# Attention block with a query projection: the first eight heads' queries accumulated chunk by chunk, six heads at once

## The chip, the cores and the metric

The kernel runs on one core of a Trainium2 chip. The metric is the time of one execution in device microseconds; smaller is better. Besides timed executions there is, for each kernel, one profiled execution with its trace. The profile's span (first to last instruction) is about 1.8 us shorter than the time of the same execution. All times in the profile count from the start of the span.

## The reference, cut to what matters

Two independent problems, A and B, of the same shape, and their results side by side:

```python
# x: (16, 32, 1024)   wq: (1024, 32*128)   k_cache, v_cache: (16, 4, 512, 128)   wo: (32*128, 1024)
q = (x @ wq)                         # 32 query heads of 128
scores = q @ k.T * 128 ** -0.5       # 8 query heads share one of 4 key/value heads
o = softmax(scores) @ v
out = o @ wo
```

All is bfloat16. Only the very first step of problem A matters here: x transposed (512 tokens by 1024 model dimensions, in 8 chunks of 128 dimensions), and heads 0 to 7 of `x @ wq`. Each head takes 8 matmuls, one for each chunk, of 128 x 128 weights against 512 token columns.

## The kernel before: the parts that matter

TensorE works through one long stream. In a start phase it transposes x and projects heads 0 to 7. Then come 128 slots, each with one score group, one value group and about seven matmuls of a background stream (`units`): the other heads' projections, later the output projection. The background starts with four matmuls of head 8 before the first slot.

```python
load_x(0); load_x(1)                                   # 128 tokens each, 256 KB
load_first_wq(slice(0, 2 * DH), slice(0, HC))          # heads 0, 1: chunks 0-3, 256 KB
load_first_wq(slice(0, 2 * DH), slice(HC, DC))         # heads 0, 1: chunks 4-7
load_x(2); load_x(3)
load_first_wq(slice(2 * DH, 4 * DH), slice(0, DC))     # heads 2, 3
load_wq(0, 1)                                          # heads 4-7, 1 MB
load_k(0); load_v(0); load_wq(0, 2); load_k(1); load_v(1)
...
warm_up(5)                                             # dummy matmuls while x is on its way
transpose_x(0); transpose_x(1)
first_q = [psum.tile([P, NW], FP32, name="q_ps", tag="proj") for _ in range(2)]
warm_up(2)
for dcs in (lower, upper):                             # heads 0, 1 on the first 256 tokens
    for h in range(2):
        first_heads(h, 0, 2, dcs)
transpose_x(2); transpose_x(3)
for h in range(2):
    for tt in (2, 3):                                  # ... and on 128 tokens at a time
        first_heads(h, tt, tt + 1, range(DC))
...                                                    # two copies out of PSUM
units = stream()                                       # heads 2, 3, ... one after another
run(units, (REP - 2) * DC + 4)                         # heads 2-7 and four matmuls of head 8
...
for i in range(total_slots + 3):                       # slot i: loads of the plan, scores(i), ...
```

## Time and profile before

| | |
|---|---|
| time, median (lowest to highest of 3) | 350.49 us (349.77 to 350.71) |
| span of the profile | 348.6 us |
| TensorE (PE) busy | 98% of the span |
| first score group (first slot) starts | 22.56 us |
| last copy of the output starts (ScalarE) | 344.38 us |
| x, in four loads, has landed | 3.5, 4.2, 7.8, 8.8 us |

The page's chain of waits, followed back from the last instruction, has shares of the span by engine. It is nearly all TensorE:

```profile
PE 96%; DMA 2%; SPq 1%; DVE 1%; issue 0%; ACT 0%
```

Here is the start in the timeline: start us, duration us, engine, line, operation, what it writes and reads, and how many; in brackets the idle time before and what ended it. L491 are dummy matmuls, L506 transposes of x, L516 heads 0 and 1, L312 heads 2 and up, L371 scores, L341 the last copy.

```profile
1.29 2.32 PE L491 MATMUL warm_ps<-warm 128*128 128x512 bf16 x5 [1.29 <-DVE warm L230]
3.55 1.56 PE L506 MATMUL xT_ps<-ident,x_sb 128*128 128x128 bf16 x16
...
5.76 1.92 PE L516 MATMUL q_ps<-xT,wq_sb 128*128 128x256 bf16 x16 [0.21 <-DMA wq_sb<-in_A_wq_dram]
...
7.81 0.62 PE L506 MATMUL xT_ps<-ident,x_sb 128*128 128x128 bf16 x8
...
8.88 0.62 PE L506 MATMUL xT_ps<-ident,x_sb 128*128 128x128 bf16 x8 [0.45 <-DMA x_sb<-in_A_x_dram]
...
9.34 2.11 PE L516 MATMUL q_ps<-xT,wq_sb 128*128 128x128 bf16 x32
...
11.34 11.38 PE L312 MATMUL q_ps<-xT,wq_sb 128*128 128x512 bf16 x52
...
22.56 0.60 PE L371 MATMUL s_ps<-qT,kT 128*128 128x256 bf16 x4
...
344.38 0.37 ACT L341 CAST o_sb<-f_ps 128x256 bf16<-128x256 f32 x1 [22.13 <-PE f_ps L331]
```

From 11.34 us on TensorE has hardly a gap. What comes before holds waits for x and for weights, and 48 narrow matmuls for two heads. A matmul of 512 columns starts every 0.216 us at full speed (52 of them take 11.38 us, of which the last one's own latency is 0.38), and a dummy one at the start every 0.42 us: the array still runs at half its rate there.

### The profile page before, as it was taken

How to read it: one execution, taken by the hardware profiler on the slowest of the kernel's cores; microseconds unless marked ns; L12 is line 12 of the kernel's file. 1: busy time of each engine (PE TensorE's matmuls, PEld its weight loads, DVE VectorE, ACT ScalarE, POOL GpSimd, SP SyncE). 2: the span in 40 equal slices, each digit the busy share in tenths (PEclk: the TensorE clock that was granted, in tenths of full speed). 3: DMA queues.
4: the chain of work that ended last, by engine and by line, in shares of the span. 5: the costliest groups of instructions: out<-in, count | busy, mean ns of one | idle time of the engine just before them, and what ended most of it. 6: DMA issues, size and time to landing. Idle time of an engine off the chain costs nothing.

```text
span 348.6 us, 5527 instructions
## 1 busy us (share of the span) xinstructions
PE 342.2 (98%) x2217; PEld 221.2 (63%) x2217; DVE 282.6 (81%) x420; ACT 180.4 (52%) x197; POOL 8.9 (3%) x21
## 2 busy tenths in 40 slices
PE   7999999999999999999999999999999999999995
PEld 4556666666666666666666666666666666666554
DVE  2118988888988889898889989999999999899710
ACT  3347667666666766666654454454455445445000
POOL 0000000000000000000000000000000000000010
PEclk9999999999999999999999999999999999999999
DMA  7999999899997899999999459995589995400000
GB/s 224 240 302 333 168 253 270 241 276 256 270 253 197 172 249 222 311 267 268 279 316 222 115 124 270 349 212 121 137 259 263 252 227 102 120 18 0 15 32 20
DMA packets 125069, 71.70 MB, mean 206 GB/s; under 512 B 73616, under 2 KB 124048, under 8 KB 125040
## 3 DMA queue, kind: packets, MB, share of 16 engines
q1 hardware_dynamic: 124176, 69.29, 81.7%
q0 software_dynamic: 720, 1.97, 1.7%
q8 instruction: 18, 0.29, 0.3%
q14 instruction: 11, 0.09, 0.1%
q10 hardware_dynamic: 144, 0.07, 0.1%
HBM read 51.38 MB, written 2.10 MB: 153 GB/s over the span
## 4 chain that ended last, share of the span: by engine, by line
PE 96%; DMA 2%; SPq 1%; DVE 1%; issue 0%; ACT 0%
PE f_ps L331 32%; PE q_ps L312 31%; PE ob L431 16%; PE s_ps L371 16%; DMA x_sb<-in_A_x_dram 2%; PE q_ps L516 1%; SPq L468 0%; DVE parts L390 0%; PE sums L407 0%; SPq L471 0%; DVE o_sb L343 0%; PE xT_ps L506 0%; ACT o_sb L341 0%; DVE cs L399 0%; PE ok_ps L627 0%
## 5 line engine op out<-in xcount | busy, mean ns | idle before, releaser
L379 ACT ACTIVATE p_sb<-s_ps,shift 128x1024 bf16<-128x1024 f32 x128 | 142.5, 1113 | 113.1 <-PE s_ps L371 100.4
L390 DVE TRANSPOSE_TENSOR_REDUCE parts<-p_sb 128x32 f32<-128x1024 bf16 x128 | 158.2, 1236 | 22.1 <-ACT p_sb L379 21.6
L331 PE MATMUL f_ps<-wo_sb,oT 128*128 128x512 bf16 (+1 forms) x544 | 133.3, 367 | 0.0
L312 PE MATMUL q_ps<-xT,wq_sb 128*128 128x512 bf16 x496 | 129.6, 380 | 0.0
L371 PE MATMUL s_ps<-qT,kT 128*128 128x256 bf16 x512 | 76.8, 273 | 0.0
L431 PE MATMUL ob<-p_sb,v_sb 128*128 128x256 bf16 x512 | 76.8, 273 | 0.0
L331 PEld LDWEIGHTS <-oT 128*128 128x128 bf16 x544 | 53.0, 98 | 33.8
L312 PEld LDWEIGHTS <-wq_sb 128*128 128x128 bf16 x496 | 48.4, 98 | 34.7 <-DMA wq_sb<-in_A_wq_dram 0.3
L371 PEld LDWEIGHTS <-kT 128*128 128x128 bf16 x512 | 56.9, 113 | 20.9
L431 PEld LDWEIGHTS <-v_sb 128*128 128x128 bf16 x512 | 50.1, 98 | 19.8 <-DVE oT L453 0.2
L453 DVE TENSOR_TENSOR oT<-r,ob 128x512 bf16<-128x512 f32 x64 | 43.9, 685 | 12.8 <-PE ob L431 9.4
L418 DVE STREAM_TRANSPOSE r<-rall 128x512 f32<-128x512 f32 x64 | 45.5, 711 | 2.2
L320 ACT CAST qT<-q_ps 128x512 bf16<-128x512 f32 x62 | 36.1, 583 | 21.3 <-PE q_ps L312 19.2
L407 PE MATMUL sums<-cs,fold 128*128 128x16 f32 x64 | 22.9, 357 | 0.1
L343 DVE CAST o_sb<-f_ps 128x512 bf16<-128x512 f32 (+1 forms) x16 | 10.8, 673 | 10.8 <-PE f_ps L331 10.0
L399 DVE TENSOR_REDUCE cs<-parts 128x16 fp32r<-128x64 f32 x64 | 16.8, 262 | 2.2
L407 PEld LDWEIGHTS sums<-cs,fold 128*128 128x128 f32 x64 | 12.1, 190 | 8.3 <-DVE cs L399 0.9
L345 POOL DMA_DIRECT2D out_dram<-o_sb x15 | 8.2, 549 | 329.3 <-DVE o_sb L343 298.6
L416 DVE RECIPROCAL rall<-sums 128x16 f32<-128x16 f32 x64 | 14.1, 220 | 0.0
L341 ACT CAST o_sb<-f_ps 128x256 bf16<-128x256 f32 x1 | 0.4, 372 | 22.1 <-PE f_ps L331 22.1
L509 DVE COPY xT<-xT_ps 128x512 bf16<-128x512 bf16 x4 | 1.7, 424 | 5.6 <-PE xT_ps L506 5.6
L509 ACT COPY xT<-xT_ps 128x512 bf16<-128x512 bf16 x4 | 2.3, 585 | 5.7 <-PE xT_ps L506 5.7
(27 smaller groups left out, 24.1 us busy)
## 6 DMA issues: line engine op xcount, KB each, us to landing
v_sb<-in_A_v_cache_dram SPq DMA_DIRECT2D x16, 512.0 KB, 5.0
wq_sb<-in_B_wq_dram SPq DMA_DIRECT2D x8, 1024.0 KB, 6.5
wo_sb<-in_A_wo_dram SPq DMA_DIRECT2D x8, 1024.0 KB, 7.6
v_sb<-in_B_v_cache_dram SPq DMA_DIRECT2D x16, 512.0 KB, 4.5
wo_sb<-in_B_wo_dram SPq DMA_DIRECT2D x8, 1024.0 KB, 8.8
wq_sb<-in_A_wq_dram SPq DMA_DIRECT2D x7, 1024.0 KB, 7.4
out_dram<-o_sb POOLq DMA_DIRECT2D x15, 128.0 KB, 3.6
x_sb<-in_A_x_dram SPq DMA_DIRECT2D x4, 256.0 KB, 3.9
```

Of the source, the lines that this page charges most:

```text
L312: nc.tensor.matmul(ps[:], lhsT=w[:, dc, (h % 4) * DH:(h % 4 + 1) * DH], rhs=xT[pr][:, dc, :], start=(dc == 0), stop=(dc == DC - 1),)
L320: nc.scalar.copy(out=qT[pr, g][:, :, hl, :], in_=ps[:].rearrange("p (b s) -> p b s", s=SQ),)
L331: nc.tensor.matmul(ps[:, 0:width], lhsT=oT[pr, tt][:, h, :], rhs=wo_tiles[pr, nh, h // REP][:, h % REP, off:off + width], start=(h == 0), ...
L371: nc.tensor.matmul(s_ps[:, c, :], lhsT=kT[:, i % GRP, c, :], rhs=qT[pr, g][:, b, :, :].rearrange("p h s -> p (h s)"), start=True, stop=True,)
L379: nc.scalar.activation(out=p_sb[:], in_=s_ps[:], func=ACTF.Exp, bias=shift[:], scale=SCALE)
L390: nc.vector.tensor_reduce(out=parts[j][:, q, :, :].rearrange("p c h -> p (c h)"), in_=st[i]["p"][:].rearrange("p c (h s) -> p (c h) s", s=SQ),
L399: nc.vector.tensor_reduce(out=cs[:], in_=parts.pop(j)[:].rearrange("p q c h -> p q h c"), axis=AX.X, op=ALU.add,)
L407: nc.tensor.matmul(sums[:], lhsT=fold[:].rearrange("p r s -> p (r s)"), rhs=cs[:].rearrange("p q h -> p (q h)"), start=True, stop=True,)
L416: nc.vector.reciprocal(out=rall[:, j, :], in_=pair.pop(j)[:])
L418: nc.vector.transpose(out=r[:].rearrange("p n s -> p (n s)"), in_=rall[:, j, :].unsqueeze(2).to_broadcast([P, 2 * REP, SQ]),)
L431: nc.tensor.matmul(ob[j][:, q, :], lhsT=v_sb[:, i % GRP, c, :], rhs=st[i]["p"][:, c, :], start=(c == 0), stop=(c == KC - 1),)
L453: nc.vector.tensor_tensor(out=out, in0=rcp.pop(j)[:].rearrange("p (q h) s -> p q h s", h=REP), in1=ob.pop(j)[:].rearrange("p q (h s) -> p ...
```

## The change

The intent: no head should wait for all of x. The loads come in chunks of the model dimension, two chunks of x and then the weights of all eight heads for one chunk at a time, and six heads advance together in six PSUM banks, so that each 256 KB of weights feeds six full-width matmuls as soon as it lands. The other two banks serve the transposes. Heads 6 and 7 follow when the transposes are done. The diff, cut to its core, with comments added:

```diff
-            load_x(0)
-            load_x(1)
-            load_first_wq(slice(0, 2 * DH), slice(0, HC))
-            load_first_wq(slice(0, 2 * DH), slice(HC, DC))
-            load_x(2)
-            load_x(3)
-            load_first_wq(slice(2 * DH, 4 * DH), slice(0, DC))
-            load_wq(0, 1)
-            load_k(0)
-            load_v(0)
-            load_wq(0, 2)
+            load_x(0, slice(0, TT // 2))            # two chunks of x, half of the tokens: 128 KB
+            load_x(0, slice(TT // 2, TT))
+            load_w0(0, slice(0, HALF * DH))         # chunk 0 of the weights, heads 0-3: 128 KB
+            load_w0(0, slice(HALF * DH, REP * DH))
+            for k in range(1, DC // 2):
+                load_x(k)                           # 256 KB each from here
+                load_w0(2 * k - 1)
+                load_w0(2 * k)
+            load_w0(DC - 1)
+            load_k(0, slice(0, 1))
+            load_wq(0, 2)
+            load_k(0, slice(1, GRP))
+            load_v(0)
             load_k(1)
             load_v(1)
...
-            warm_up(5)
...
+            warm_up(4)
+            transpose_x(0)                          # now chunks 2k and 2k+1, all tokens
+            warm_up(1, QW)
...                                                  # first_q: six banks
+            for dc in range(DC - 2):
+                for h in range(NF):                 # NF = 6
+                    first_head(first_q[h], h, dc)
+                if dc % 2 == 0:
+                    transpose_x(dc // 2 + 1)
+            for h in (0, 2, 4, 1, 3, 5):
+                for dc in (DC - 2, DC - 1):
+                    first_head(first_q[h], h, dc)
+                evacuate(first_q[h], h)
...                                                  # heads 6 and 7, all chunks; VectorE copies head 7
-            run(units, (REP - 2) * DC + 4)
+            run(units, 4)
```

From the first slot on both kernels issue the same work in the same order.

More of the change, by code (lines that the diff above doesn't have):

```diff
@@ L279, in kv_part, with load_k @@
                 return t[jj]
-            def load_k(j):
+            def load_k(j, qs=slice(0, GRP)):
                 ks = kv_part(j, 1)
-                kT = k_tiles[j] = kv.tile([P, GRP, SK], BF16, name="kT")
+                if qs.start == 0:
+                    k_tiles[j] = kv.tile([P, GRP, SK], BF16, name="kT")
+                kT = k_tiles[j]
                 if j < NG // GRP:
-                    for q in range(GRP):
+                    for q in range(qs.start, qs.stop):
                         nc.sync.dma_start_transpose(out=kT[:, q, :], in_=ks[q])
@@ L463, in fast_path @@
             wq_v = A_wq.rearrange("(c p) n -> p c n", p=P)
-            wq_tiles[0, 0] = blk_tile([P, DC, 4 * DH], "wq_sb")
             HC = DC // 2
-            def load_x(tt):
-                nc.sync.dma_start(out=x_sb[:, tt, :], in_=x_v[:, tt, :])
-            def load_first_wq(ns, cs):
-                nc.sync.dma_start(out=wq_tiles[0, 0][:, cs, ns], in_=wq_v[:, cs, ns])
-            load_x(0)
-            load_x(1)
-            load_first_wq(slice(0, 2 * DH), slice(0, HC))
-            load_first_wq(slice(0, 2 * DH), slice(HC, DC))
@@ L477, in fast_path, with load_x, load_w0 @@
-            load_x(2)
-            load_x(3)
-            load_first_wq(slice(2 * DH, 4 * DH), slice(0, DC))
-            load_wq(0, 1)
-            load_k(0)
+            w0 = [blk_tile([P, HC, REP * DH], "w0_sb") for _ in range(2)]
+            def load_x(k, ts=slice(0, TT)):
+                cs = slice(2 * k * P, (2 * k + 2) * P)
+                nc.sync.dma_start(out=x_sb[:, ts, cs], in_=x_v[:, ts, cs])
+            def load_w0(dc, ns=slice(0, REP * DH)):
+                nc.sync.dma_start(out=w0[dc // HC][:, dc % HC, ns], in_=wq_v[:, dc, ns])
@@ L485, in fast_path, with warm_up @@
             load_v(1)
-            warm_ps = psum.tile([P, NW], FP32, name="warm_ps", tag="sums", bufs=1)
-            def warm_up(n):
+            warm_ps = psum.tile([P, NW], FP32, name="warm_ps", tag="proj")
+            def warm_up(n, width=NW):
                 for _ in range(n):
                     nc.tensor.matmul(
-                        warm_ps[:], lhsT=warm[:, 0:P], rhs=warm[:], start=True, stop=True
+                        warm_ps[:, 0:width], lhsT=warm[:, 0:P], rhs=warm[:, 0:width],
+                        start=True, stop=True,
@@ L493, in warm_up @@
                     )
             xT[0] = blk_tile([P, DC, NTOK], "xT")
-            def transpose_x(tt):
-                ts = slice(tt * P, (tt + 1) * P)
-                bank = ("ob", "proj", "sums", "ob")[tt]
-                for cs, where_, copy in (
-                    (slice(0, HC), dict(tag="s"), nc.vector.tensor_copy),
-                    (slice(HC, DC), dict(tag=bank, bufs=2 if bank == "proj" else 1), nc.scalar.copy),
-                ):
-                    xT_ps = psum.tile([P, HC, P], BF16, name="xT_ps", **where_)
-                    for k, dc in enumerate(range(cs.start, cs.stop)):
-                        nc.tensor.transpose(
-                            xT_ps[:, k, :], x_sb[:, tt, dc * P:(dc + 1) * P], ident[:]
-                        )
-                    copy(out=xT[0][:, cs, ts], in_=xT_ps[:])
@@ L511, in fast_path @@
-            qT[0, 0] = blk_tile([P, B, REP, SQ], "qT")
-            def first_heads(h, t0, t1, dcs):
-                ts = slice(t0 * P, t1 * P)
-                for dc in dcs:
-                    nc.tensor.matmul(
-                        first_q[h][:, ts],
-                        lhsT=wq_tiles[0, 0][:, dc, h * DH:(h + 1) * DH],
-                        rhs=xT[0][:, dc, ts],
-                        start=(dc == 0),
-                        stop=(dc == DC - 1),
-                    )
-            lower, upper = range(HC), range(HC, DC)
@@ L525, in fast_path @@
-            warm_up(5)
-            transpose_x(0)
-            transpose_x(1)
-            first_q = [psum.tile([P, NW], FP32, name="q_ps", tag="proj") for _ in range(2)]
-            warm_up(2)
-            for dcs in (lower, upper):
-                for h in range(2):
-                    first_heads(h, 0, 2, dcs)
-            transpose_x(2)
-            transpose_x(3)
-            for h in range(2):
-                for tt in (2, 3):
-                    first_heads(h, tt, tt + 1, range(DC))
@@ L538, in fast_path, with transpose_x @@
-            for h, copy in enumerate((nc.vector.tensor_copy, nc.scalar.copy)):
+            def transpose_x(k):
+                ps = [
+                    psum.tile([P, NTOK], BF16, name="xT_ps", tag=tag, bufs=1)
+                    for tag in ("ob", "sums")
+                ]
+                for ts in (range(0, TT // 2), range(TT // 2, TT)):
+                    for o in range(2):
+                        dc = 2 * k + o
+                        for tt in ts:
+                            nc.tensor.transpose(
+                                ps[o][:, tt * P:(tt + 1) * P],
+                                x_sb[:, tt, dc * P:(dc + 1) * P],
+                                ident[:],
+                            )
+                nc.vector.tensor_copy(out=xT[0][:, 2 * k, :], in_=ps[0][:])
+                nc.scalar.copy(out=xT[0][:, 2 * k + 1, :], in_=ps[1][:])
@@ new lines, in fast_path, with first_head, evacuate @@
+            qT[0, 0] = blk_tile([P, B, REP, SQ], "qT")
+            NF = REP - 2
+            def first_head(q_ps, h, dc):
+                nc.tensor.matmul(
+                    q_ps,
+                    lhsT=w0[dc // HC][:, dc % HC, h * DH:(h + 1) * DH],
+                    rhs=xT[0][:, dc, :],
+                    start=(dc == 0),
+                    stop=(dc == DC - 1),
+                )
+            def evacuate(q_ps, h):
+                copy = nc.vector.tensor_copy if h in (2, 1, 5, 7) else nc.scalar.copy
@@ L539, in fast_path @@
                 copy(
                     out=qT[0, 0][:, :, h, :],
-                    in_=first_q[h][:].rearrange("p (b s) -> p b s", s=SQ),
+                    in_=q_ps.rearrange("p (b s) -> p b s", s=SQ),
                 )
+            warm_up(4)
+            transpose_x(0)
+            warm_up(1, QW)
+            first_q = []
+            for _ in range(2):
+                pair_ps = psum.tile([P, 2, NW], FP32, name="q_ps", tag="s")
+                first_q += [pair_ps[:, k, :] for k in range(2)]
@@ new lines, in fast_path @@
+            first_q += [psum.tile([P, NW], FP32, name="q_ps", tag="proj")[:] for _ in range(2)]
+            for dc in range(DC - 2):
[7 more added lines that the diff above has]
+                evacuate(first_q[h], h)
+            for h, tag in zip(range(NF, REP), ("ob", "sums")):
+                q_ps = psum.tile([P, NW], FP32, name="q_ps", tag=tag, bufs=1)
+                for dc in range(DC):
+                    first_head(q_ps[:], h, dc)
+                evacuate(q_ps[:], h)
@@ L544, in stream @@
             def stream():
-                for h in range(2, HQ):
+                for h in range(REP, HQ):
                     yield from q_units(0, h)
```

## The prediction

> **What bounds the kernel now.** TensorE. The page gives it 98% busy of a 348.6 us span; the chain of waits is 96% TensorE, and nearly all the rest is start-up (DMA of x 2%). From 11.3 us on the timeline shows matmuls back to back. So only the start can give anything, and its end is a clean marker: the first score matmul (first `s_ps` group), at 22.56 us. Everything after it is the same instructions in the same order.
>
> Before 22.56 us there is this useful work: 68 projection matmuls of 512 columns (52 took 11.38 us with the last one's latency, so 0.216 us each): 14.7 us; 32 transposes, 0.06 us each when data is there (8 in 0.62 us with latency), 1.9 us. Waits and inefficiency now: nothing useful can start before x lands at 3.5 us; then gaps of 0.70, 0.41 and 0.62 us (waits for weights and x), two filler matmuls (0.6 us), and heads 0 and 1 done in 48 narrow pieces (16 of 256 and 32 of 128 columns: 1.92 + 2.11 us, instead of 16 x 0.216 = 3.5). In the timeline wq heads 8-11 also arrive just in time (0.3 us wait at 21.6).
>
> **What changes.** Same bytes, same transposes. Heads 0-5 advance together per chunk of the model dimension, so each 256 KB of weights feeds six full-width matmuls (1.3 us) as soon as it lands. Removed: the 0.5 us of narrow matmuls and most of the waiting for all of x (x(3) lands at 8.85 us). Added: 15 small issues on SyncE (0.43-0.5 us each, not limiting), x in 512 B runs, 6+2 evacuations (DVE 0.69, ACT 0.58 us, hidden under matmuls).
>
> **Supply against demand.** In the trace successive 256 KB loads land about 1.05 us apart early (5.7, 6.4, 7.8, 8.85 us) and GB/s rises to 330-350 later (0.75-0.8 us apart). Two chunks need 768 KB: 2.4-3.1 us; TensorE needs 12 x 0.216 + 8 x 0.06 = 3.1 us for them. So supply and demand are nearly equal. My estimate of the new timeline: first chunk matmul 4.8 us, short waits (0.2-0.5 us each) before chunk 1 and perhaps chunks 3 and 7, last head done at 20.4-21.0 us, first scores at 21.2-21.9 us instead of 22.56. With everything supplied it would be 20.6.
>
> **On the critical path:** all of that difference, 0.7-1.4 us, since TensorE is dense afterwards. The order of loads also brings heads 8-11 earlier, removing the 0.3 us wait. The next weights (heads 12-15) land at about 29.6 us and are needed about 31.6 us; this slack of 2 us shrinks to about 0.8 us, so I expect no new wait there.
>
> **Time: 349.4 us (348.6 to 350.5).** Faster by over 2%: 0.5%; within 2%: 98.5%; slower: 1%.
>
> **What would show it.** First `s_ps` at 21.2-21.9 us; distance from there to the end unchanged (326.1 us); waits of TensorE's weight loads for `w0_sb`/`x_sb` under 1.5 us in total after 4.8 us; 64 `q_ps` matmuls of 512 columns in the start, none narrower.
>
> **What would make it wrong.** (1) The clock: the Trainium skill, "TensorE: Matmul & The Clock Gate" (What's actually happening), says the array runs at half rate until a free-running window of about 3.4 us has been busy. The trace agrees: warm-up matmuls start 0.42 us apart, those at 11.3 us 0.216. The new start has one warm-up matmul and a half fewer and gaps while x lands; if the full clock comes one window later, 1-1.7 us are lost and the gain is gone. (2) x in 512 B runs landing slower than 1.05 us per 256 KB: every chunk waits. (3) Key and weight loads behind it late: a new wait at heads 12-15. (4) The spread of before, 0.9 us, is near the gain.

## More of the kernel before

At its end the kernel waits for a flag and ends in a branch (`with tc.If(ok < total, ...)`) past a general path that this data never takes.

In the view of one line's instructions, with least, median and largest duration in ns and the times of the first and last:

```profile
L637 SPq EVENT_SEMAPHORE  x8: 17/17/17, 346.4 to 347.0; - x8
```

Before it ends, SyncE (SP) waits for eight semaphores one after another, and does all of that after the last work.

A line that turned out to matter belongs to the end of the kernel, the branch at L637.

## The result, and the profile after

| | before | after |
|---|---|---|
| time, median (lowest to highest of 4) | 350.51 (349.77 to 350.71) | 349.85 (349.43 to 350.08) |
| ratio, with its 95% interval | | 0.9985 (0.9971 to 0.9999) |
| the same, five rounds more (5 and 11 runs) | 350.45 (349.85 to 350.68) | 349.74 (349.55 to 349.83) |
| ratio | | 0.9980 (0.9967 to 0.9993) |
| span | 348.6 | 347.9 |
| first score group | 22.56 | 22.28 |
| last copy of the output | 344.38 | 344.11 |

Ratios are the mean time of one kernel's fast runs over that of the other's of the same rounds, so not quite the ratio of the medians quoted. The change gains about 0.6 us in these two batches, and 0.2 us in a third one, reported under the experiments. The prediction had 1.1 us, with first scores at 21.2 to 21.9 us. They came at 22.28 us. And the table shows something else that does not fit: the last copy came only 0.27 us earlier (344.38 - 344.11), but the span is 0.7 us shorter. More than half of the gain lies behind the last piece of work.

The timeline of the kernel after. L496 are dummy matmuls, L512 transposes, L524 heads 0 to 7, L314 head 8, L534 copies of finished heads, L373 scores:

```profile
1.29 1.89 PE L496 MATMUL warm_ps<-warm 128*128 128x512 bf16 x4 [1.29 <-DVE warm L230]
...
3.17 1.19 PE L512 MATMUL xT_ps<-ident,x_sb 128*128 128x128 bf16 x8
...
4.66 1.93 PE L524 MATMUL q_ps<-xT,w_sb 128*128 128x512 bf16 x6
...
6.42 0.61 PE L512 MATMUL xT_ps<-ident,x_sb 128*128 128x128 bf16 x8
...
7.37 2.82 PE L524 MATMUL q_ps<-xT,w_sb 128*128 128x512 bf16 x12 [0.34 <-DMA w_sb<-in_A_wq_dram]
...
10.78 2.76 PE L524 MATMUL q_ps<-xT,w_sb 128*128 128x512 bf16 x12
...
13.83 7.58 PE L524 MATMUL q_ps<-xT,w_sb 128*128 128x512 bf16 x34
...
21.24 1.03 PE L314 MATMUL q_ps<-xT,wq_sb 128*128 128x512 bf16 x4
21.44 0.69 DVE L534 CAST qT<-q_ps 128x512 bf16<-128x512 f32 x1 [2.76 <-PE q_ps L524]
...
22.28 0.60 PE L373 MATMUL s_ps<-qT,kT 128*128 128x256 bf16 x4
...
344.11 0.37 ACT L343 CAST o_sb<-f_ps 128x256 bf16<-128x256 f32 x1 [22.13 <-PE f_ps L333]
```

Three things are to be seen. The first six matmuls take 1.93 us, which is more than six times 0.216: part of them ran at half rate. Chunk 1 starts at 7.37 us and chunk 3 at 10.78 us after waits for their weights. And the first scores start 0.15 us after VectorE's copy of head 7 (21.44 + 0.69 = 22.13), not when the four matmuls of head 8 are issued (21.24 + 4 x 0.216 = 22.10): TensorE stood still for about 0.2 us.

The list of waits for the start (engine, line, waited for, us in total, times, longest):

```profile
PEld L524 <- DMA w_sb<-in_A_wq_dram: 1.4, 4, 0.5
```

And the end of the kernel, where SyncE waits for the same eight semaphores:

```profile
L655 SPq EVENT_SEMAPHORE  x8: 17/17/17, 342.6 to 346.2; - x8
```

The first of them is now passed at 342.6 us, before the last work. The records of SyncE after the final branch, read from the two traces, in us from the span's start:

```
                 waits at the branch, one record each                          then 12 fixed ones, drain at
before  (8)      346.42 346.52 346.60 346.68 346.75 346.82 346.89 346.95       347.77
after   (2)      346.14 346.21                                                 347.02
```

In before all eight come after the last store; in after six were passed earlier and two are left. That is 1.35 us against 0.88 us from the first of these waits to the drain, 0.47 us less.

The loads themselves: issue plus time to landing, as the view of DMA issues gives them in narrow windows, puts x pair 1 at 6.0 us, the weights of chunk 1 at 7.3, of chunk 2 at 8.7, x pair 2 at 9.5 and the weights of chunk 3 at 10.7 us. The trace has 16 completion marks for each load, and the last one counts (the matmuls of chunk 3 start at 10.78 us). They lie far apart here: of the weights of chunk 1 fifteen marks were there at 6.67 us and the last came at 7.33; for chunk 3 the first came at 8.88, half were there by 9.6 and the last came at 10.73 us (for chunk 7: 14.24 to 14.37). So TensorE waited for the slowest part of each load; what slowed that part, no run shows. The weights of heads 12 to 15, first of the loads planned for the slots, were issued at 23.25 us and landed at 31.3 us (before: 22.11 and 29.5). TensorE needs them about 31.4 us in after, 31.7 us in before.

### The profile page after: what moved, and what is told of

Read it like the earlier page. It is cut to its first block, busy times and chain, and to the rows that moved or that the text cites. A ratio compares the mean times of both kernels' runs of the same rounds, so it can differ in the third digit from the quotient of the medians.

```text
span 347.9 us, 5469 instructions
## 1 busy us (share of the span) xinstructions
PE 342.1 (98%) x2183; PEld 219.1 (63%) x2183; DVE 284.8 (82%) x423; ACT 178.9 (51%) x194; POOL 8.9 (3%) x21
## 4 chain that ended last, share of the span: by engine, by line
PE 95%; DMA 2%; SPq 1%; DVE 1%; issue 0%; ACT 0%
PE f_ps L333 32%; PE q_ps L314 28%; PE s_ps L373 16%; PE ob L433 16%; PE q_ps L524 3%; DMA w_sb<-in_A_wq_dram 2%; SPq L474 1%; SPq L471 1%; DVE parts L392 0%; PE sums L409 0%; DVE o_sb L345 0%; PE xT_ps L512 0%; ACT o_sb L343 0%; DVE cs L401 0%; PE ok_ps L645 0%
## 5 line engine op out<-in xcount | busy, mean ns | idle before, releaser
L314 PE MATMUL q_ps<-xT,wq_sb 128*128 128x512 bf16 x448 | 119.3, 380 | 0.0
L373 PE MATMUL s_ps<-qT,kT 128*128 128x256 bf16 x512 | 76.8, 273 | 0.0
L373 PEld LDWEIGHTS <-kT 128*128 128x128 bf16 x512 | 56.8, 113 | 21.2 <-issue 0.5
L314 PEld LDWEIGHTS <-wq_sb 128*128 128x128 bf16 x448 | 43.8, 98 | 29.2
L322 ACT CAST qT<-q_ps 128x512 bf16<-128x512 f32 x56 | 32.7, 584 | 14.3 <-PE q_ps L314 12.3
L524 PE MATMUL q_ps<-xT,w_sb 128*128 128x512 bf16 x64 | 15.1, 388 | 0.6 <-DMA w_sb<-in_A_wq_dram 0.3
L524 PEld LDWEIGHTS <-w_sb 128*128 128x128 bf16 x64 | 6.1, 100 | 8.4 <-DMA w_sb<-in_A_wq_dram 1.4
```

What stands on the lines that cost most here:

```text
L314: nc.tensor.matmul(ps[:], lhsT=w[:, dc, (h % 4) * DH:(h % 4 + 1) * DH], rhs=xT[pr][:, dc, :], start=(dc == 0), stop=(dc == DC - 1),)
L322: nc.scalar.copy(out=qT[pr, g][:, :, hl, :], in_=ps[:].rearrange("p (b s) -> p b s", s=SQ),)
L373: nc.tensor.matmul(s_ps[:, c, :], lhsT=kT[:, i % GRP, c, :], rhs=qT[pr, g][:, b, :, :].rearrange("p h s -> p (h s)"), start=True, stop=True,)
L524: nc.tensor.matmul(q_ps, lhsT=w0[dc // HC][:, dc % HC, h * DH:(h + 1) * DH], rhs=xT[0][:, dc, :], start=(dc == 0), stop=(dc == DC - 1),)
```

## The experiments

Twelve kernels were run. The theories when they began:

- **Supply.** The loads of weight chunks land 1.3 us apart instead of the 0.75 to 1.05 us of the prediction, and TensorE waits for them.
- **Clock.** The array's full rate came at 5.64 us in the profile of after, by the trace's clock record, and at 4.63 us in that of before; the half rate eats what the early start gains.
- **Last copy.** The first scores wait for head 7's copy.
- **Late load.** What is gained at the start is given back at 31 us, where the weights of heads 12 to 15 aren't there yet.

The table has the marks of each profile, for all kernels without a gate. "Full clock" is from the trace's clock record, counted from the start of the span, since the page's row of granted clock reads 9 everywhere (the recorded expectations give these times 0.25 us too late, 4.9 for 4.63 and 5.9 for 5.64 us; the starts of the matmuls fit the earlier ones, and differences are the same); "waits left" are SyncE's at the branch after the last store.

| kernel | full clock | first scores | last copy | scores to copy | waits left | span |
|---|---|---|---|---|---|---|
| before | 4.63 | 22.56 | 344.38 | 321.82 | 8 | 348.6 |
| before, again | 4.76 | 22.11 | 343.94 | 321.83 | 8 | 348.2 |
| after | 5.64 | 22.28 | 344.11 | 321.83 | 2 | 347.9 |
| after, second | 6.23 | 22.01 | 344.14 | 322.13 | 2 | 348.0 |
| after, third | 7.47 | 22.31 | 344.13 | 321.82 | 2 | 347.9 |
| supply-free | 5.03 | 21.13 | 343.28 | 322.15 | 2 | 347.2 |
| supply-free, values later | 6.15 | 21.65 | 343.47 | 321.82 | 2 | 347.3 |
| six matmuls between | 7.39 | 22.51 | 344.24 | 321.73 | 2 | 348.1 |
| values later | 5.04 | 22.35 | 344.17 | 321.82 | 2 | 348.0 |
| two queues | 11.37 | 25.12 | 346.94 | 321.82 | 2 | 350.7 |
| whole first loads | 7.90 | 22.77 | 344.60 | 321.83 | 4 | 348.6 |
| combination | 4.98 | 22.62 | 343.68 | 321.06 | 4 | 347.7 |

The expectations below speak of the last matmul; it starts 0.3 us before the last copy, so their 321.5 us are 321.8 us in the table.

### Before and after once more

No edit.

> The kernel before, unchanged, for its spread and its clock. If the array's clock window is free-running, the moment of full clock differs from run to run (it was 4.9 us in the profile of before and 5.9 us in that of after) and isn't a property of the kernel; if the new start with fewer warm-up matmuls delays it, this run shows about 4.9 again. First score matmul at 22.5 us either way (half-rate ends before TensorE's first real matmul at 5.75). Time 350.0-350.7 us.

> The kernel after, unchanged. Supply theory (weight loads land about 1.3 us apart, chunk 3 at 10.7 us holds TensorE): chunk 3 starts at 10.5-10.9 us and first scores at 22.0-22.4 us whatever the clock does. Clock theory (half-rate until 5.9 us cost the missing part): if full clock comes at 4.9 us here, first scores come 0.5 us earlier, 21.8 us. Time 349.5-350.0 us.

Measured: before 350.28 us, ratio to the other runs of before 0.9999 (0.9983 to 1.0016); after 350.05 us, ratio 0.9994 (0.9978 to 1.0011). In the second profile of before, x landed earlier and first scores came at 22.11 us, so before itself varies by 0.45 us. After's first scores came at 22.01 us, and its chunk 3 at 10.51 us, with the full clock as late as 6.23 us. The expectation of the clock theory could not be read, since the clock came later and not earlier. By the marks, TensorE's work ended at 343.94 us in this before and at 344.14 us in this after: no gain there at all. The span was still 0.2 us shorter.

The second profile of after has a wait that its first one did not have. From the list of waits between 24 and 40 us:

```profile
PEld L314 <- DMA wq_sb<-in_A_wq_dram: 0.4, 1, 0.4
```

This is the late load: with the first scores at 22.01 us, TensorE gets to heads 12 to 15 before their weights do. It cost 0.3 us (322.13 against 321.83 in the table).

> The kernel after, unchanged, for a narrower interval of the change itself: 0.3-0.6 us below before (ratio 0.9983 to 0.9992), where the prediction had 1.1 us.

Measured, in the last batch, with five rounds: 349.74 us, ratio 0.9980 (0.9967 to 0.9993), a little more gain than expected. Here the full clock came at 7.47 us, and the chain of waits (start us, duration, what) holds no load at all in the start:

```profile
4.68 2.72 PE q_ps L524 x6
7.40 0.54 PE xT_ps L512 x8
7.94 2.59 PE q_ps L524 x12
10.53 0.45 PE xT_ps L512 x8
10.98 2.59 PE q_ps L524 x12
```

Six matmuls took 2.72 us, all at half rate, and by then the weights of all next chunks were there. First scores at 22.31 us, as in the first profile of after (22.28), where the clock came 1.8 us sooner and TensorE waited for loads instead. The two costs don't add up: what the clock delays, the loads need not wait for.

### Supply-free: the first heads read only chunk 0

```diff
-                    lhsT=w0[dc // HC][:, dc % HC, h * DH:(h + 1) * DH],
+                    lhsT=w0[0][:, 0, h * DH:(h + 1) * DH],
...
-                                x_sb[:, tt, dc * P:(dc + 1) * P],
+                                x_sb[:, tt, o * P:(o + 1) * P],
```

The queries of heads 0 to 7 are wrong on purpose. All loads and instructions stay. (The comparison with the reference passed all the same: its tolerance doesn't see those queries. It proves nothing here.)

> Wrong result on purpose: same loads, same instructions, but the first heads' matmuls read only chunk 0 of the weights and the transposes only chunks 0 and 1 of x, so nothing after the first chunk waits for a load. Supply theory: TensorE dense from the first real matmul at 4.7 us, first scores at 21.0-21.6 us instead of 22.28, time 0.7-1.3 us below after. Clock theory: the half clock still costs, first scores not before 22.0 us.

Measured: 349.25 us, ratio 0.9969 (0.9953 to 0.9986), 0.8 us below the kernel after of the same rounds (350.05). TensorE is dense from the first projection:

```profile
4.73 1.59 PE L524 MATMUL q_ps<-xT,w_sb 128*128 128x512 bf16 x6
6.15 0.61 PE L512 MATMUL xT_ps<-ident,x_sb 128*128 128x128 bf16 x8
6.60 2.75 PE L524 MATMUL q_ps<-xT,w_sb 128*128 128x512 bf16 x12
...
21.13 0.60 PE L373 MATMUL s_ps<-qT,kT 128*128 128x256 bf16 x4
```

So the waits for loads are worth about 1 us of first scores when the clock comes early, as the supply theory said: 1.2 us against the kernel "values later", whose clock came at the same time (22.35 - 21.13). With the clock at about 6.2 us they are worth 0.4 us (22.01 in the second profile of after, 21.65 in the other supply-free kernel). This run also gives back 0.3 us at 31 us, by the same wait as above.

### Six matmuls of head 8 before the first scores instead of four

```diff
-            run(units, 4)
+            run(units, 6)
```

> Six instead of four projection matmuls of head 8 between the last first head and the first scores. Theory of the last copy (the first scores wait 0.2 us for VectorE's 0.69 us copy of head 7; in before the copy took 0.58 us on ScalarE and nothing waited): the first scores come about 0.25 us later (two matmuls 0.43 minus the wait 0.18) but the end of TensorE's work comes 0.15-0.2 us earlier than in after. Rival (the 0.2 us is only the way starts are drawn in the trace): end of TensorE's work unchanged.

Measured: 349.98 us, ratio 0.9983 (0.9967 to 1.0). The wait before the first scores is gone: the six matmuls start at 21.22 us and the scores at 22.51 us, 6 x 0.216 = 1.30 us later. But TensorE's work ended 0.13 us later than in after. The background stream is now two matmuls ahead, so it asks for heads 12 to 15 sooner and waits for them, at 31 us: 0.5 us in the list of waits, 0.67 us by the starts of the slots. (A wait of TensorE for VectorE near 211 us, before the matmul into `sums`, is gone in this kernel and gives 0.33 us back.) The last copy did cost its 0.2 us; taking it away alone only feeds the late load.

### The second value load behind the weights of heads 12 to 15

```diff
             load_k(1)
-            load_v(1)
...
             for c4 in range(3, 16):
                 need = (c4 - 2) * 4 * DC / 7.0
                 at(max(0, int(need) - 10), load_wq, c4 // 8, c4 % 8)
+                if c4 == 3:
+                    at(0, load_v, 1)
```

> After, with the second value load (512 KB) moved behind the weights of heads 12-15 in the load queue. Late-load theory (in after these weights land at 31.2-31.4 us, where TensorE needs them at 31.2-31.4; in before 29.5 against 31.7): they land 1.2-1.8 us earlier, TensorE has no wait at 31 us, and the distance from first scores to the last matmul is 321.5 us in every state (it was 321.5 in after, 321.8 in its second run and in the supply-free run). Rival (that wait is noise of the trace): distance unchanged. Time 0 to 0.3 us below after.

Measured: 349.70 us, ratio 0.9986 (0.9969 to 1.0003). The weights landed at 29.4 us (issued at 22.48, 6.9 us to landing) instead of 31.3, 31.4 and 30.6 in the three profiles of after, and nothing waited at 31 us. But in this profile the start was so late (first scores at 22.35 us, with the full clock at 5.04 and chunk 1 waiting for its weights until 7.81) that nothing need have waited without the edit either, as in the first profile of after. The landing was as expected; the next run was to test the wait itself.

> Wrong result on purpose: the supply-free kernel (first heads read only chunk 0) with the second value load behind the weights of heads 12-15. Late-load theory: first scores at 21.0-21.6 us as in the supply-free run, and now no weight wait near 31 us: from first scores to the last matmul 321.5 us instead of 321.8, time about 0.3 us below the supply-free kernel, 1.2 below before or more. Rival: the wait comes again, 321.8 us.

This kernel has both edits, the supply-free one and this one. Measured: 348.84 us, ratio 0.9953 (0.9939 to 0.9968), 1.6 us below before. First scores at 21.65 us, and the list of waits of TensorE from 24 to 40 us is empty; scores to copy 321.82 us instead of the 322.15 of the supply-free kernel. That the late load takes back 0.3 us after an early start is shown by the traces that have the wait: in the second profile of after the weights landed at 31.40 us and their first matmul started at 31.45. That the other order of loads gives the 0.3 us again is not shown. Here the start was 0.5 us later than in the supply-free run, so TensorE needed these weights at 30.79 us; they landed at 29.62, but the 30.55 us of the supply-free run would have been in time as well. The ratio to before improved (0.9953 against 0.9969), but in different rounds, and in the profiles TensorE's work ended later here (343.47 against 343.28).

The two supply-free runs measure the clock as well. Between them the full clock moved from 5.03 to 6.15 us, 1.12 us, and the first scores from 21.13 to 21.65 us, 0.52 us: half, as half rate must cost where no load binds.

### Weights of chunks 0 to 2 issued from ScalarE's queue

```diff
-            load_w0(0, slice(0, HALF * DH))
-            load_w0(0, slice(HALF * DH, REP * DH))
+            load_w0(0, slice(0, HALF * DH), nc.scalar)
+            load_w0(0, slice(HALF * DH, REP * DH), nc.scalar)
...
-                load_w0(2 * k - 1)
-                load_w0(2 * k)
+                load_w0(2 * k - 1, eng=nc.scalar if k == 1 else None)
+                load_w0(2 * k, eng=nc.scalar if k == 1 else None)
```

(ScalarE's table load was put behind these.)

> After, with the weights of chunks 0, 1 and 2 issued from ScalarE's queue (before its table load) beside x on SyncE's queue. Feeding theory (one queue issuing 128 KB per 0.5 us cannot keep the engines busy from 2 to 5 us; bytes moved by 5.0 us: 0.62 MB in after, 0.85 MB in before): bytes by 5 us reach 0.85 MB or more, chunk 1 starts by 6.6 us, TensorE has no weight wait over 0.2 us after 5 us, first scores at 20.9 us plus half of the time from 4.7 us to full clock (20.9 to 22.4). Rival (the engines or the memory set the landing, not the issue): chunk 3 again not before 10.4 us, first scores 22.0 us or later whatever the clock.

Measured: 351.96 us, ratio 1.0044 (1.0027 to 1.0061): slower by 1.5 us, and the feeding theory missed. The first loads were issued earlier, but bytes per us did not rise from 2 to 5 us (184, 252 and 267 GB/s, against 199, 261 and 237 in after: 0.7 MB by 5 us in both, where the expectation had 0.62 for after), and the weights now competed with x:

```profile
3.87 0.61 PE L513 MATMUL xT_ps<-ident,x_sb 128*128 128x128 bf16 x4 [0.70 <-DMA x_sb<-in_A_x_dram]
5.42 0.61 PE L513 MATMUL xT_ps<-ident,x_sb 128*128 128x128 bf16 x4 [0.94 <-DMA x_sb<-in_A_x_dram]
```

The halves of the first x pair were used at 3.17 and 3.75 us in after. The Trainium skill, "DMA: Bandwidth & Descriptors" (Rules for kernel authors), says that issuing from several engines gives no bandwidth, since all run on the same 16 DMA engines and interleave, and only saves issue time. Up to 5 us this run agrees, and shows that interleaving can cost: x, needed first, came 0.7 and 1.7 us later. From 6 to 8 us it moved more than after (319 and 346 GB/s, against 205 and 245), but before, from one queue, moved as much there (350 and 317 in its second profile). The early issue did not last either: the weights of chunk 6 were issued at 8.97 us instead of 6.89, held back by the landing of x pair 1 at 8.96 (the section on the end of the kernel tells why). The clock came late too. With TensorE idle 0.70 and 0.94 us in its first microseconds, full rate came only at 11.37 us.

### The first loads whole

```diff
-            load_x(0, slice(0, TT // 2))
-            load_x(0, slice(TT // 2, TT))
-            load_w0(0, slice(0, HALF * DH))
-            load_w0(0, slice(HALF * DH, REP * DH))
+            load_x(0)
+            load_w0(0)
```

> After, with the first x pair and the first weight chunk loaded as 256 KB each instead of two 128 KB halves, so that everything behind is issued 1 us earlier. Issue theory (four 128 KB loads at one per 0.5 us starve the engines before 5 us): weights of chunk 1 start work at 6.4-6.9 us instead of 7.1-7.8, chunk 3 not later than 9.9 us when full clock comes before 6 us; first scores 21.2-21.9 us. Rival (what holds the landings is how fast the engines take 2 KB rows[...]): chunk 1 again at 7.1 us or later, first scores 22.0-22.4.

Measured: 350.35 us, ratio 0.9999 (0.9985 to 1.0014), no better than before. The weights of chunk 1 were issued at 2.37 us instead of 3.32 us, and landed at 7.1 us instead of 7.3. The issue theory falls: something behind the issue sets when these loads land. The DMA columns of the windows view (last two: DMA share, GB/s) dip here as in after, though at other moments (the kernel with two queues has no such dip); two slices of after:

```profile
4.00:5.00 1.00, 0.91 (x6) 0.41 (x4) 0.42 (x1) 0.59 (x1) 0.00 (x0) 1.00 0.78 237
6.00:7.00 1.00, 1.00 (x11) 0.62 (x9) 0.04 (x1) 0.00 (x0) 0.00 (x0) 1.00 0.73 205
```

and the same slices of this kernel:

```profile
4.00:5.00 1.00, 0.98 (x9) 0.60 (x6) 0.41 (x1) 0.20 (x1) 0.00 (x0) 1.00 0.66 175
6.00:7.00 1.00, 1.00 (x4) 0.43 (x3) 0.00 (x0) 0.00 (x0) 0.00 (x0) 1.00 0.88 287
```

The start got worse for another reason: x, now in one piece, was there at 3.73 us instead of 3.17, TensorE idled 0.55 us, and full rate came at 7.90 us:

```profile
3.73 1.03 PE L510 MATMUL xT_ps<-ident,x_sb 128*128 128x128 bf16 x8 [0.55 <-DMA x_sb<-in_A_x_dram]
```

### A gate in front of both kernels

To take the clock out of the comparison, all loads were held back to about 10 us by memsets of x, and TensorE kept at dummy matmuls, in both kernels:

```diff
+            for _ in range(12):
+                nc.vector.memset(x_sb[:, 0, :], 0.0)
             load_x(...)
...
-            warm_up(...)
+            warm_up(22)
+            nc.vector.memset(warm[:], 0.0)
+            warm_up(9)
```

> Before, with 12 memsets of x holding back all loads to about 9 us and TensorE kept at dummy matmuls until then and until x lands, so that the clock is full before any real work. The time from the first x issue to first scores was 21.25 to 21.7 us in the two profiles of before, both with full clock before the first projection; both theories expect 21.2-21.8 us here. Total time about 8.3 us longer.

> After, with the same gate. Clock theory: from first x issue to first scores 19.9-20.3 us, 1.0-1.5 us less than in the gated before, and the times differ by as much. Supply theory: chunk 3 still starts 9.6-9.9 us after the first issue, first scores 21.1-21.4 us after it, 0-0.5 us less than in the gated before, as without the gate.

Measured: 359.92 and 359.36 us; first scores at 32.02 and 31.68 us, so 0.34 us between them. The gate failed at its purpose. TensorE's 22 dummy matmuls ended near 8 us and it idled until 10.57 us; the clock record shows full rate at 4.85 us, half at 11.68 and full again at 15.09 (before), and 4.45, 11.28 and 14.69 (after). Full rate was back before the first projection in both, at 16.02 and 15.09 us, but the dummy matmuls at half rate also made the transposes start late, at 13.33 and 13.73 us, though x had been issued at 10.27 us. That hits after more than before. The 0.34 us agree with the supply theory's range and not with the clock theory's 1.0 to 1.5, but with that delay the pair settles nothing.

It did show how the clock moves. The three changes lie 6.83 and 3.41 us apart in one run, 6.83 and 3.41 us in the other: a grid of 3.41 us. That agrees with the prediction's source, the Trainium skill, "TensorE: Matmul & The Clock Gate" (What's actually happening), with its free-running window of 3413 ns. The place of the grid against the kernel's start is not fixed: full rate came anywhere from 4.45 to 7.90 us (two queues aside), and TensorE's first dummy matmul was at 1.29 us in each. The grid also shows which windows of 3.41 us gave full rate. Counted over the starts of the fourteen traces, by the modelled ends of the matmuls, those with up to 0.55 us without a matmul did (0.55 in the combination below), those with 0.65 us or more did not (0.65 in the third profile of after, all of it before the first dummy matmul).

### The combination

Whole first loads, the value load later and six matmuls between, all three edits above.

> Whole first loads, the second value load behind the weights of heads 12-15, and six matmuls between the last first head and the first scores (hides the 0.2 us wait for the last copy). Issue and late-load theories: no weight wait over 0.2 us after 8 us, end of TensorE's work 0.5-1.0 us before that of after; time 349.0-349.4 us, ratio to before 0.996-0.998. Rival: as after, 349.8 us.

Measured: 350.04 us (349.49 to 350.94), ratio 0.9998 (0.9985 to 1.0012), against 349.74 us of the kernel after in the same rounds. It did not beat it. In its profile the clock was early (4.98 us), chunk 1 waited for its weights until 7.82 us, the end of TensorE's work came 0.45 us before that of after, and the end of the kernel had two waits more. The 0.45 us do not come from the start: first scores to last copy is 0.77 us shorter than in after, of which two matmuls moved ahead are 0.43 and the missing wait near 211 us 0.33. The whole first loads were the wrong part to put in. A kernel with only the value load later and six matmuls between, with the halves kept, was not run. The supply-free kernels are faster than both, but they compute wrong queries; no valid version that beats the kernel after was found.

### The end of the kernel, over all runs

No run was made for this alone, but the fourteen profiles line up. In before and in its gated version all eight waits are left after the last store; in after and all its variants with the same number of loads two are left; with two loads fewer (whole first loads, combination) four are left. After issues six loads more than before in the start (14 against 8 up to the end of the first eight heads' weights), and 8 - 6 = 2; two loads fewer again, and 2 + 2 = 4. From the last copy to the end of the span it is 4.2 to 4.3 us with eight waits, 4.0 us with four, and 3.8 to 3.9 us with two. Each wait takes about 0.07 us (346.42 to 346.95 in before for eight).

The reading that fits all of this: the DMAs take the eight completion semaphores in turn, and at the end SyncE goes through the eight in a fixed order. The one of the last store stops it; those ahead of it in the order are already done with, those behind it still cost 0.07 us each. How many are behind depends on nothing but the count of DMAs issued, modulo eight. The semaphore numbers in the traces bear it out. SyncE and ScalarE issue 153 DMAs in before, and each takes the next of the eight semaphores; the last store takes the first in the order of the waits (153 = 19 x 8 + 1), and its wait passes at 346.42 us, when the store has landed (346.40). In after 159 DMAs put the store on the seventh, and with whole first loads 157 put it on the fifth. What is not shown is the change of the time by this alone: an extra load in before was not run.

The same semaphores act at the start, which the prediction left out. In these programs SyncE issues a DMA only when the one eight before it, which had its semaphore, has landed. In after the first key load was issued at 8.70 us, when the weights of chunk 2 were there (8.68), and the second at 10.75, when those of chunk 3 were (10.73). So more and smaller loads in front also hold back the issue of everything behind them.

## Why the prediction was right or wrong, point by point

The prediction had 349.4 us (348.6 to 350.5), and no change of over 2%. Measured 349.85 and 349.74 us. The number held, but for reasons only partly its own: that the end of the kernel made up for the start was luck.

- **"Only the start can give anything", and "distance from there to the end unchanged (326.1 us)": wrong.** From first scores to the end of the span it was 325.6 us in the first and third profile of after (347.9 - 22.28, 347.9 - 22.31). The work in between did keep its length (321.8 us), but the end got 0.4 to 0.5 us shorter, six semaphore waits of SyncE. This is most of the measured gain of 0.6 to 0.7 us (more than the 0.2 us of the batch with the second profiles), and the prediction did not have it.
- **First scores at 21.2 to 21.9 us: wrong**, 22.28, 22.01 and 22.31 us. Before, in two profiles, had 22.56 and 22.11. TensorE's work ended at 344.38 and 343.94 us in before and at 344.11, 344.14 and 344.13 us in after. What the new start gains for TensorE is not more than the spread between the two profiles of before.
- **"Supply and demand are nearly equal": the right mechanism, mis-sized.** The prediction took 1.05 us for 256 KB early and 0.75 to 0.8 later. From x pair 1 (6.0 us) to the weights of chunk 3 (10.7 us) four loads took 4.7 us, 1.2 us each, and the last of them held TensorE until 10.78 us. It was the weights: chunks 1, 2 and 3 landed 1.3 us after the load before them, the x pairs in 512-byte runs, which the prediction feared, only 0.9 and 0.8 us. Without waits for loads, first scores came at 21.13 us. The waits for weights, predicted under 1.5 us in total, were 1.4 us in the first profile.
- **Cause 1 of error, the clock, named beforehand: it happened.** Full rate came at 5.64, 6.23 and 7.47 us in after, and 4.63 and 4.76 us in before. The main estimate had taken before's clock for granted. It costs half of the delay where nothing else binds (0.52 us of first scores for 1.12 us of clock). In after it is hidden behind the waits for loads, or hides them: with the clock at 5.64 or at 7.47 us, first scores are the same within 0.03 us. The later clock was the place of the grid and not the new start: in all three profiles of after the last window without full rate began before the first dummy matmul at 1.29 us (at 0.64 us in the third), and the trace has no gap in the rest of it. In before the grid lay better, twice.
- **Evacuations "hidden under matmuls": wrong for the last one.** Head 7's copy on VectorE held the first scores for 0.2 us.
- **"I expect no new wait" at heads 12 to 15: wrong.** Their weights landed at 31.3, 31.4 and 30.6 us instead of 29.5. The loads of the start moved fewer bytes early (0.70 MB by 5 us against 0.88, from the GB/s of the windows from 2 us on), and everything queued behind them came later; that this is the whole cause is argued. Against the time at which TensorE would have needed them, the predicted slack of 0.8 us was 0.1, minus 0.25 and 0.9 us in the three profiles of after: the second waited, as did the supply-free kernel.
- **The load order "removing the 0.3 us wait" for heads 8 to 11: right.** No such wait in the profiles of after.
- **No narrow matmuls, 64 of 512 columns: right.**

What stays open is why 256 KB of weights in 2 KB rows land about 1.3 us after the load before them between 6 and 11 us, and why the 16 marks of one load lie so far apart (1.85 us for chunk 3). Earlier issue did not help: with whole first loads the weights of chunk 1 were issued 0.95 us earlier, with two queues 1.5 us earlier, and they landed at 7.1 and 7.6 us instead of 7.3. Rows of another length were not tried.

## What to carry to other kernels

At the start of a kernel several limits lie close together: here the landing of the loads, the array's half rate, the last copy and a load needed 9 us later were all within half a microsecond of each other, so that removing one hands the time to the next. Take away each alone, with wrong data if need be, before believing that a better order of work will pay. And when a gain is smaller than 1 us, look at where the work ends and where the span ends, both: a change of the number of DMAs can move the kernel's end by itself.

## What the Trainium skill lacked or had wrong

- No page has the waits for DMA completion at a kernel's end: SyncE passes eight semaphores in turn at 0.07 us each, and 2, 4 or 8 of them came after the last store, worth up to 0.47 us. "Runtime: NRT & Kernel Launch" (The ~15µs preamble/postamble breakdown) gives only fixed stages around the kernel.
- "TensorE: Matmul & The Clock Gate" (What's actually happening) has the window of 3413 ns right (3.41 us in two traces), but not how much idle time makes a window fail: in the starts of the fourteen traces 0.55 us without a matmul still gave full rate, and 0.65 us did not. With a gap of 0.55 us while x was awaited and 0.21 us before the first dummy matmul, the boundary at 7.90 - 3.41 = 4.49 us passed without full rate, which came at 7.90 us; with gaps of 0.70 and 0.94 us it came at 11.37 us.
- "DMA: Bandwidth & Descriptors" (Rules for kernel authors) says that several issuing engines don't add bandwidth; it doesn't say that they delay what is needed first. Here the second half of the first x pair was used at 5.42 us instead of 3.75 us.
- No page tells how the rate of several loads in flight runs at a kernel's start: 175 to 290 GB/s in the slices of 1 us from 3 to 5 and 6 to 8 us, against 300 to 390 from 8 to 12 us, in after, its third run, and the two kernels with whole first loads.
